# Identity products in TensorE's waits of the first slots, and a rounding that needs one PSUM bank

## The chip, the cores and the metric

The kernel runs on one core of a Trainium2 chip. The metric is device time in microseconds of one execution, as the median of several runs. The engines are TensorE (PE for its products, PEld for its weight loads), VectorE (DVE), ScalarE (ACT), GpSimd (POOL) and SyncE (SP), which here only issues DMAs. [...]

## The reference

Two layers in a row, in f32. The first is a recurrence of 768 steps on a 40 x 40 state for each of 4 x 8 heads; the second is a feed-forward network (FFN) with squared ReLU on the 3072 tokens that come out.

```python
for t in range(S):                                   # S = 768, B = 4, H = 8, D = 40
    y[:, :, t] = np.einsum('bhd,bhde->bhe', rt, state)
    Sa = np.einsum('bhde,bhe->bhd', state, at)
    state_decay = state * wt[:, :, None, :] - np.einsum('bhd,bhe->bhde', Sa, bt)
    state = state_decay + np.einsum('bhd,bhe->bhde', vt, kt)
...
x = np.ascontiguousarray(attn_out.transpose(0, 2, 1, 3)).reshape(B * S, H * D)   # 3072 x 320
h = np.maximum(x @ w_in, 0.0)                        # w_in 320 x 2048
return (h * h @ w_out).astype(np.float32)            # w_out 2048 x 320
```

The two weight matrices are made from random numbers times a factor, so they are f64: two 32-bit words for each element. The other inputs are f32.

## The kernel before

The recurrence is cut into chunks of 128 steps: 6 chunks for each of 4 batches, 24 in all, taken in the order of `order` (all batches of a chunk first). Within a chunk the steps are solved together, which needs the inverse of a triangular 128 x 128 matrix for each head.

For a chunk, `early` (or `prepare` around it) turns w, b and a on TensorE (`turn`, line 318), makes running products of w by scans and two reciprocals on VectorE (lines 354 to 360), multiplies (366, 367) and makes the matrices N with products of 40 rows (`products`, line 326). ScalarE copies them to SBUF (375 to 379), and they are stored in DRAM. GpSimd fetches them (`take`), inverts small triangles step by step (`solving`, lines 442 to 452), and stores the result as kept_t (455). `inverses` fetches that back as blocks (472), and joins it into T: a transpose on VectorE (484), two rounds of 32 x 32 products on TensorE, copies on ScalarE (486, 496, 503). `chain` is the recurrence proper: in_v,A products, then xr,T and minus_x,N products by turns with ScalarE's copies between, a transpose (635), the masked RX (645), and the products that make the tokens (661) and the new state. `turn_rv`, `make_rv`, `turn_k`, `turn_down` and `scale_kb` prepare r, v and k for it; `turn_down` transposes the decays, and VectorE multiplies k and b by them (552).

A slot is the work on one chunk woven with the preparation of others. Slots 0 to 3 are `opening_slot`, which has no FFN in it; from slot 4 on it is `sorted_slot`, with the FFN's steps between: `thirds` and `whole` (the first layer: w_third and w_in products into two ps_f banks), `square` (line 726) and `make_quarter` (the second layer). After slot 23 `rest` does what is left of the FFN. The order of all engines' work is the order in which these steps are called. `later`, `tick` and `flush` delay the issue of stores and fetches by a number of steps; nearly all of them go through SP's queue, and GpSimd issues its own.

The weights come as f64 and are rounded to f32 on the chip by `rounding`, in 26 pieces: 10 of 512 columns (w_in and w_third) and 16 of 320 (w_out). The raw words are fetched into lent space in SBUF (w_out's place, the hidden tiles). For each piece ScalarE turns the low words into a fraction (line 264); VectorE takes the exponent (277) and the mantissa (278) from the high words into two PSUM banks and adds the fraction (279); in the next step ScalarE makes a power of two of the exponent (260), and VectorE puts in the sign (268) and multiplies (269). Then a further fetch may use the raw space (`then`, line 239). `thirds` may start when the first 10 pieces are done, and `make_quarter` when all are. The pieces are dealt to the slots by `pieces_in` (line 867): 3, 6, 6 and 9 in slots 0 to 3, and 3 in slot 4, the last of which only ends the piece before.

[...]4 in the pool ps_w, 2 in ps_c, and 2 in ps_f, which the rounding uses until slot 4 and the FFN after it:

```python
bits, mant = (psum(ps_f)[:, :dst.shape[-1]] for _ in range(2))
```

Ahead of the loop, the first four chunks are prepared (`e0` to `e3`), the first chunk's own preparation is `r0`, and `solve` 0, 1 and 2 are GpSimd's first three units, of 1, 1 and 2 chunks.

## Time and profile before

| | us |
|---|---|
| median of 3 runs (lowest, highest) | 973.73 (973.63, 974.14) |
| the profiled execution | 973.32 |
| its span, first to last instruction | 971.5 |

| engine | busy, us | share of the span | instructions |
|---|---|---|---|
| PE | 874.8 | 90% | 9008 |
| PEld | 725.8 | 75% | 9008 |
| DVE | 477.4 | 49% | 872 |
| ACT | 284.7 | 29% | 735 |
| POOL | 512.4 | 53% | 993 |

| stretch, us | PE busy | DVE busy | granted PE clock |
|---|---|---|---|
| 50 to 100 | 34.19 | 27.36 | 0.57 |
| 100 to 150 | 32.82 | 38.21 | 0.60 |
| 150 to 200 | 39.63 | 39.04 | 0.59 |
| 200 to 250 | 29.69 | 31.35 | 0.69 |
| 250 to 300 | 47.40 | 28.81 | 0.97 |
| 300 to 350 | 48.83 | 29.16 | 1.00 |

Slot 0 begins with the join of T for chunk 0 at 58.7 us, slot 1 at about 91 us, slot 2 at 130, slot 3 at 170, and slot 4 at 214.5, as the transposes of in_r show; the first FFN product comes at 230.0. In the profile a group is named by its output and inputs, so "PE ps_w L318" is a transpose into a bank of the pool ps_w, and "ps_c<-xr,T" a product whose operands are xr and T. An f32 product is two PE instructions. The granted clock is the share of full speed at which TensorE's array was allowed to run.

### The profile page before, as it was taken

The numbers are of one execution on the slowest core, as the hardware profiler recorded it, in microseconds if no ns is written. First come the engines' busy times: TensorE is split into PE (matmuls) and PEld (weight loads), VectorE is DVE, ScalarE is ACT, GpSimd is POOL, SyncE is SP. The second block draws the span as 40 slices with busy tenths as digits, with TensorE's granted clock in tenths as the row PEclk, the third lists the DMA queues.
The fourth block names the chain that finished last, engine by engine and source line by source line (L and its number), as shares of the span: only waits on it lengthen the run. The fifth ranks groups of instructions, "written<-read, shape, count | busy, mean of one in ns | idle before, by whom it ended". The sixth has DMA issues, their size and how long they took to land.

```text
span 971.5 us, 22220 instructions
## 1 busy us (share of the span) xinstructions
PE 874.8 (90%) x9008; PEld 725.8 (75%) x9008; DVE 477.4 (49%) x872; ACT 284.7 (29%) x735; POOL 512.4 (53%) x993
## 2 busy tenths in 40 slices
PE   6457856755989999999999999999999999999998
PEld 4446745654868878788878888888888888887776
DVE  5527975876466556536644644644334323231111
ACT  3133432433332423323323422222222221222111
POOL 4788327064183846029999739999858860000000
PEclk9856565566999999999999999999999999999999
DMA  8989997874566897884772796525454353130000
GB/s 101 147 167 142 173 173 174 185 136 85 100 116 117 148 170 134 145 152 87 120 109 70 147 157 118 107 44 85 98 118 80 55 107 67 32 51 8 14 14 13
DMA packets 256313, 103.67 MB, mean 107 GB/s; under 512 B 237236, under 2 KB 243252, under 8 KB 255060
## 3 DMA queue, kind: packets, MB, share of 16 engines
q1 hardware_dynamic: 251892, 86.92, 51.4%
q0 software_dynamic: 3232, 15.21, 6.9%
q8 instruction: 71, 1.16, 0.5%
q10 hardware_dynamic: 1088, 0.13, 0.1%
q14 instruction: 30, 0.25, 0.1%
HBM read 69.33 MB, written 30.92 MB: 103 GB/s over the span
## 4 chain that ended last, share of the span: by engine, by line
PE 75%; DVE 8%; DMA 5%; issue 4%; SPq 3%; POOL 3%; ACT 2%; DVEq 0%; ACTq 0%; POOLq 0%
PE ps_f L87 40%; PE ps_w L87 15%; PE ps_c L87 12%; PE ps_w L318 5%; DMA blocks<-kept_t 2%; PE ps_c L635 1%; PE ps_c L562 1%; POOL half_t L452 1%; POOL half_p L450 1%; SPq L144 1%; PE ps_w L546 1%; DVE decay L359 1%; DMA kept_q<-N 1%; DMA kept_t<-half_t 1%; DMA w_out<-in_moe_w_in_dram 1%
## 5 line engine op out<-in xcount | busy, mean ns | idle before, releaser
L450 POOL TENSOR_TENSOR half_p<-half_n,half_t 128x126 f32<-128x126 f32 (+44 forms) x437 | 225.0, 515 | 95.2 <-DMA half_n<-kept_q 30.2
L452 POOL TENSOR_TENSOR half_t<-half_t,half_p 128x126 f32<-128x126 f32 (+44 forms) x437 | 241.9, 553 | 34.2
L87 PE MATMUL ps_f<-w_out,hid 128*128 128x320 f32 x768 | 222.5, 442 | 0.0
L87 PEld LDWEIGHTS ps_f<-w_out,hid 128*128 128x128 f32 x768 | 143.8, 193 | 54.8 <-issue 2.5
L87 PE MATMUL ps_f<-tokens,w_in 128*128 128x256 f32 x672 | 156.9, 387 | 0.0
L87 PEld LDWEIGHTS ps_f<-tokens,w_in 128*128 128x128 f32 x672 | 126.2, 193 | 17.8 <-issue 1.0
L726 DVE TENSOR_TENSOR hid<-hid 128x512 f32<-128x512 f32 x96 | 81.5, 886 | 50.2 <-ACT hid L719 49.7
L719 ACT ACTIVATE hid<-ps_f 128x512 f32<-128x512 f32 x84 | 50.2, 597 | 86.1 <-PE ps_f L87 86.1
L422 POOL DMA_DIRECT2D half_n<-kept_q x18 | 9.4, 528 | 102.6 <-DMA kept_m<-N 55.4
L661 DVE TENSOR_TENSOR tokens<-ps_c,dec 128x512 f32<-128x512 f32 x24 | 16.6, 691 | 90.2 <-PE ps_c L87 90.2
L354 DVE TENSOR_TENSOR_SCAN decay<-ps_w,ones 128x64 f32<-128x64 f32 x88 | 23.9, 272 | 72.8 <-PE ps_w L318 72.8
L87 PE MATMUL ps_w<-decay,bT 40*128 40x128 f32 x352 | 31.7, 314 | 26.4 <-DVE decay L367 26.1
L87 PE MATMUL ps_f<-tokens,w_third 64*128 64x256 f32 x336 | 46.6, 385 | 8.0 <-DVE w_out L268 8.0
L87 PEld LDWEIGHTS ps_w<-decay,bT 40*128 40x128 f32 x352 | 28.6, 219 | 30.4 <-DVE decay L367 21.7
L375 ACT COPY N<-ps_w 128x256 f32<-128x256 f32 x48 | 17.7, 369 | 112.4 <-PE ps_w L87 69.9
L512 DVE TENSOR_TENSOR kvT<-ps_w,dec 128x512 f32<-128x512 f32 x24 | 16.5, 687 | 68.8 <-ACT minus_x L622 34.4
L334 DVE TENSOR_TENSOR RV<-ps_w,upper 128x512 f32<-128x512 f32 x48 | 30.9, 686 | 38.8 <-PE ps_w L87 38.5
L334 DVE TENSOR_TENSOR RX<-ps_w,upper 128x512 f32<-128x512 f32 x48 | 30.8, 684 | 35.4 <-PE ps_w L87 35.2
L87 PEld LDWEIGHTS ps_c<-xr,T 64*64 64x64 f32 x768 | 29.9, 146 | 19.9 <-issue 15.3
L87 PE MATMUL ps_w<-spares 32*32 32x32 f32 x448 | 11.9, 208 | 32.9 <-DVE spares L484 17.5
L87 PEld LDWEIGHTS ps_f<-tokens,w_third 64*128 64x128 f32 x336 | 31.7, 190 | 10.3 <-DVE w_out L268 8.3
L87 PE MATMUL ps_c<-xr,T 64*64 64x40 f32 x768 | 35.9, 240 | 2.7 <-ACT xr L629 1.6
(130 smaller groups left out, 1422.9 us busy)
## 6 DMA issues: line engine op xcount, KB each, us to landing
kept_e<-decay SPq DMA_DIRECT2D x22, 633.8 KB
dec<-kept_e SPq DMA_DIRECT2D x22, 633.8 KB
hid<-in_moe_w_out_dram SPq DMA_DIRECT2D x16, 320.0 KB
in_w<-in_w_dram SPq DMA_DIRECT2D x24, 160.0 KB
in_ab<-in_b_dram SPq DMA_DIRECT2D x24, 160.0 KB
in_ab<-in_a_dram SPq DMA_DIRECT2D x24, 160.0 KB
in_k<-in_k_dram SPq DMA_DIRECT2D x24, 160.0 KB
in_r<-in_r_dram SPq DMA_DIRECT2D x24, 160.0 KB
```

Source lines behind the costliest of these rows:

```text
L87: nc.tensor.matmul(o, l_, r_, start=start, stop=True, skip_group_check=True)
L144: nc.sync.dma_start(out=t_[:, :, :D], in_=src[bb, :, c * C:(c + 1) * C, :].rearrange("h t d -> t h d"))
L318: nc.tensor.transpose(p_[:, q * 128:(q + 1) * 128], pair(x_, q), ident)
L334: nc.vector.tensor_tensor(t_, p_, over4(upper), Alu.mult)
L354: nc.vector.tensor_tensor_scan(up[:, q, MID + 1:C + 1], wT[:, q, MID:], ones, 1.0, Alu.mult, Alu.mult)
L375: nc.scalar.copy(plain, p_[:, ::2].rearrange("s h (f t) -> s f h t", f=2))
L450: nc.gpsimd.tensor_tensor(p_, part[:, at:at + m_].unsqueeze(1).to_broadcast([128, n, m_]), t3[:, :n, s:s + 1].to_broadcast([128, n, m_]), ...
L452: nc.gpsimd.tensor_tensor(t3[:, :n, s + 1:], t3[:, :n, s + 1:], p_, Alu.subtract)
L512: nc.vector.tensor_tensor(kT, kT_, down[:, :, 1:C + 1], Alu.mult)
L661: nc.vector.tensor_tensor(t_, y_, g["up"][:, :, :C], Alu.mult)
L719: nc.scalar.activation(h_, p_.rearrange("p f t -> p (f t)"), Act.Relu)
L726: nc.vector.tensor_tensor(h_, h_, h_, Alu.mult)
```

## The change

A new function, `fill_in(cols)`, issues products of the identity with itself, repeated along the columns, up to 4 x 128 columns in one product, into a PSUM bank that nobody reads. It is called 7 times ahead of the loop, 5 times in each opening slot, and twice in slot 4 (B is 4). Its bank, and one for the rounding, are taken once from the pool ps_f, so the rounding has one bank where it had two: the mantissa goes into the low words of the raw data in SBUF, the sum is made in place in the destination, and the sign is put into the bank instead of the destination.

```diff
+    bits_bank, fill_bank = psum(ps_f), psum(ps_f)
+
+    def fill_in(cols):
+
+        while cols:
+            n = min(4, cols)
+            nc.tensor.matmul(fill_bank[:, :n * 128], ident, ident.unsqueeze(1).to_broadcast([128, n, 128]),
+                             start=True, stop=True, skip_group_check=True)
+            cols -= n
+
     def rounding():
...
             if before:
-                d_, hi, mant, bits = before
-                nc.vector.scalar_tensor_tensor(d_.bitcast(I32), hi, -(1 << 31), bits, Alu.bitwise_and, Alu.bitwise_or)
-                nc.vector.scalar_tensor_tensor(d_, mant, 2.0 ** -20, d_, Alu.mult, Alu.mult)
+                d_, hi, bits = before
+                nc.vector.scalar_tensor_tensor(bits, hi, -(1 << 31), bits, Alu.bitwise_and, Alu.bitwise_or)
+                nc.vector.scalar_tensor_tensor(d_, d_, 2.0 ** -20, bits.bitcast(FP32), Alu.mult, Alu.mult)
...
                 hi = words[:, :, 1].bitcast(I32)
-                bits, mant = (psum(ps_f)[:, :dst.shape[-1]] for _ in range(2))
-                bits = bits.bitcast(I32)
+                low, bits = words[:, :, 0].bitcast(I32), bits_bank[:, :dst.shape[-1]].bitcast(I32)
                 nc.vector.tensor_scalar(bits, hi, 20, 0x7FF, Alu.logical_shift_right, Alu.bitwise_and)
-                nc.vector.tensor_scalar(mant.bitcast(I32), hi, 0xFFFFF, 0x100000, Alu.bitwise_and, Alu.bitwise_or)
-                nc.vector.tensor_tensor(mant, mant.bitcast(I32), dst, Alu.add)
-                now = dst, hi, mant, bits
+                nc.vector.tensor_scalar(low, hi, 0xFFFFF, 0x100000, Alu.bitwise_and, Alu.bitwise_or)
+                nc.vector.tensor_tensor(dst, low, dst, Alu.add)
+                now = dst, hi, bits
...
+    fill_in(4)
     go(e0, 3)
     go(e1)
+    fill_in(4)
     go(e0)
...
     go(e1)
+    fill_in(3)
     go(r0, 2)
...
     go(e3, 2)
+    fill_in(10)
     go(e2)
     go(e3, 2)
+    fill_in(14)
     flush()
     join = inverses(0, ready[0])
     go(join)
     go(e3)
+    fill_in(52)
     flush()
     solve(1, {8: lambda: weights_by(0, nc.gpsimd), 20: lambda: take(2, own)})
...
         fill("f")
+        fill_in(4)
         if j == 2:
             join()
         step(of(turn_k))
         step(on(ch))
+        fill_in(2)
         step(of(turn_down), of(scale_kb), pieces)
...
         step(lambda: begin_chain(j, n))
+        fill_in(12)
         fill("n")
+        fill_in(4)
         if late:
             join()
         step(pieces)
+        fill_in(3)
         if late:
             join()
...
         step(of(turn_rv), on(one), on(one))
+        if i == B:
+            fill_in(10)
         fetch_next(j + 1, "r")
         step(second.make_quarter, pieces)
         step(on(ch), of(decay_state))
+        if i == B:
+            fill_in(10)
         step(pieces, of(make_rv), second.thirds)
```

## The prediction

> **What bounds the kernel now.** I read the page first, then the chain of waits, then stretches of 10 us, then the timelines of TensorE, VectorE, ScalarE and the SP queue from 0 to 300 us.

> ```profile
> PE   6457856755989999999999999999999999999998
> DVE  5527975876466556536644644644334323231111
> POOL 4788327064183846029999739999858860000000
> PEclk9856565566999999999999999999999999999999
> ```

> Each digit is a slice of 24.3 us. From the tenth slice on (about 230 us) PE is full and its clock granted in full: the tail is TensorE's own work, which the change doesn't touch. Before that PE is half busy at half clock, and something else sets the pace. What, differs from place to place:

> ```profile
> 76.75 3.44 DMA kept_t<-half_t
> ...
> 106.04 0.69 DVE RV L334
> 106.78 1.11 PE ps_w L318 x4
> ...
> 132.13 7.36 SPq L144
> ...
> 229.49 0.50 DVE w_out L268
> 230.04 2.59 PE ps_f L87 x7
> ```

> That is the chain (start, us, what). Up to 91 us it is GpSimd's solves and their round trips through DRAM; in slot 1 (91 to 130) VectorE, busy 93% of the time from 100 to 130, much of it with the rounding; in slot 2 (130 to 153) the SP queue, which waits 7.36 us for TensorE's in_ab transposes; then TensorE and VectorE in turn; in slots 3 and 4 mostly VectorE's rounding, until the last w_out piece lets the FFN start at 230.

> The clock matters more finely than in slices:

> ```profile
> 74.88:78.30 3.42, 3.42 (x34) 3.20 (x32) 2.72 (x5) 0.00 (x0) 2.57 (x10) 0.50 1.15 148
> 78.30:81.70 3.40, 3.40 (x52) 3.40 (x48) 2.44 (x4) 1.24 (x2) 2.54 (x9) 0.50 0.33 60
> 81.70:81.80 0.10, 0.10 (x8) 0.10 (x6) 0.00 (x0) 0.00 (x0) 0.10 (x2) 0.88 0.49 83
> 88.50:88.60 0.10, 0.10 (x4) 0.06 (x1) 0.00 (x0) 0.00 (x0) 0.05 (x1) 0.76 1.72 182
> 119.20:119.30 0.10, 0.10 (x6) 0.10 (x4) 0.10 (x1) 0.10 (x1) 0.00 (x0) 0.65 1.42 277
> 122.70:126.10 3.40, 0.00 (x0) 0.00 (x0) 3.26 (x7) 0.72 (x2) 0.00 (x0) 1.00 0.95 194
> 126.00:126.10 0.10, 0.00 (x0) 0.00 (x0) 0.10 (x1) 0.10 (x1) 0.00 (x0) 0.99 0.07 26
> 238.70:238.80 0.10, 0.10 (x2) 0.06 (x2) 0.00 (x0) 0.00 (x0) 0.00 (x0) 0.81 0.00 0
> ```

> The columns are stretch, length, PE, PEld, DVE, ACT, POOL, clock, DMA share, GB/s. The last column but two of each short stretch dates a change within it: 81.72, 88.55, 119.27, 126.10 and 238.74. The gaps are 2, 9, 2 and 33 times 3.413 us. [...]78.3 to 81.7, filled with RX and in_v,in_k products, raised it; 74.9 to 78.3, PE also "busy", did not[...].[...] The first 30 us show 1.0 only for want of a record: the in_ab transposes take 421 ns at 5 us and 273 ns after 245, so TensorE is cold there too.

> [...]here windows full of transposes (214.8 to 218.2) do raise the clock, so I count them. [...]the trace shows the hid squares (L726, two SBUF inputs) at a median of 687 ns from 245 to 300 us but 1204 ns from 400 to 500, where GpSimd's operations are larger.

> **The fills, price.** A filling product is a full f32 product of 128 rows. The tokens,w_in products (8 of 256 columns, 3.46 us warm) give 1.69 ns a column: 0.216 us for each unit of 128 columns warm, 0.432 cold. There are 87 units ahead of the loop, 25 in each of slots 0 to 3, 20 in slot 4: 207, or 45 us warm and 89 cold. Nothing reads the bank, so each costs only what TensorE would have done sooner.

> **Ahead of the loop.** The first 4 (1.73 cold) fit between ident (2.55) and in_w (4.24); they overrun by 0.1 at most. [...]the next 4 lie in the idle 2.57 before 11.44. Then the first N products (2.13 us on the chain, cold) take about half: -1.0, and GpSimd's whole row of solves starts that much sooner. The 3 lie in an idle 1.33; 10 (2.2) in 3.0 at 32 us; 14 (3.0) in 3.7; 52 (11.2) in 15.4. Unknown: whether 4 units hold the clock to 11.4. Bounds -1.2 to +0.3; I take -1.0.

> **Slot 0.** The 4 and 2 in its middle are cold, 2.6 us, and together with three dense transposes raise the clock some 7 us sooner, but slot 1 waits for GpSimd's blocks at 91: 0. The 12+4+3 at the end lie in waits and leave TensorE warm at 92.

> **Slot 1.** The 4 hide in the 2.26 us for RV; the 2 sit before turn_down's transposes, whose products VectorE waits for (L552, 0.52 idle now): +0.3 at most. Warm products spare its waits of 0.65 (A) and some tenths: -0.7. VectorE has nothing else to gain. -0.4.

> **Slot 2.** The 19 units at the end of slot 1 run as one block (4.1 warm) from 122, then TensorE idles to 130 for blocks: [...]cold at 130 as now. The in_ab transposes that the SP queue waits for end at 139.7 unchanged; the queue then issues for 14 us whatever TensorE does. [...]154.5 to 167 stays cold. 0; bounds -4 (warm from 130: half of 9.2 busy) to +0.5.

> **Slot 3.** The 19 units before it move its in_r and in_v transposes from 170 to about 174.7. ScalarE takes them in order: its rT copy starts at 174.52 now behind the rounding's two steps, so it waits 0.1 to 0.3, and the minus_x copy and the rounding behind it likewise; VectorE hardly. In the middle, 4 and 2 cost up to 2.6 cold beside in_k, xnT and dec transposes, which are followed by VectorE's kvT and L552; the same dense stretch raises the clock at 184 to 187.5 in place of 197.8. VectorE's waits from 189 to 196 are 1.40 (RX), 1.04 (A) and 1.02 (scans), 3.5 in all, and nearly go. Bounds -3.5 to +2.2; I take -2.2, some of the cost being felt.

> **Slot 4.** The 12 at the end of slot 3 hide in 9.9 us of idle time, but are over seven us before the N products at 212.5, which stay cold. 7 units then stand before in_r and in_v (3.0 cold); ScalarE's rT copy starts at 219.65 now and they end at about 219. The two tens take 2.2 each, warm after 218; rT,kvT ends at about 225.7, and the FFN waits for the rounding until 230. [...]the FFN starts cold and rises at about 238, as now. 0; bounds -4.4 (warm at once: half of 8.7 busy us) to +2.6.

> **The rounding.** As many instructions as before, 5 on VectorE and 2 on ScalarE for each of 26 pieces. Line 278 into SBUF at a stride of two words: L268 wrote SBUF at 676 to 690 ns, L277 PSUM at 684: equal. It must now follow ScalarE's read of the low words (L264), which ends over a microsecond earlier. Line 279 with two SBUF inputs: between 0 and +0.2 (L726's 892 ns maximum from 300 to 400 us, against 687) for each, 5 at most; I take +0.3 in all. The first FFN bank now comes free with L269, not L268: +0.5 at 230.

> **Sum.** -1.0 -0.4 -2.2 +0.3 +0.5 = -2.8 on the profiled execution's 973.32 (span 971.5 and 1.8 around it): 970.5; the median of the runs lies 0.4 above: 970.9.

> **The rivals.**
> 1. The clock holds into the FFN, or slot 2 starts warm: another -4.4 or -4, about 966.5. For: the tens are just ahead of it. Against: the 4.3 us gap.
> 2. Absorbed: VectorE at 93%, GpSimd and the SP queue keep their times and the gains in slot 3 are eaten by the fills there: 973.5.
> 3. Slower: [...]the fills run cold on TensorE's path. Slot 1 pays 0.85, slot 3 2.2; in slot 4, from 212.5, 2.1 products, 3.0 and 8.6 of fills and 6.4 of slot work end at 232.6, past the 230 at which the FFN is free: 2.6. With 0.5 for the bank, +6.2: 979.9.[...]
> 4. That it doesn't do what it says: products of an identity might not count as activity. It gives rival 3's time.

> **How the numbers follow.** Mine 0.41, rival 1 0.17, rival 2 0.22, rivals 3 and 4 together 0.20. About 0.2% (2 us) is what a measurement can tell here. Faster: 0.32 of mine, 0.17, and 0.03 of rival 2: 0.52. Same: 0.08 and 0.16: 0.24. Slower: 0.01, 0.03 and 0.20: 0.24. My own range is 968 to 974; with the rivals, and the bounds of slots 2 to 4, 964 to 977.5.

> **What would show it.** Right: the clock at 1.0 from about 7 us and again from the middle of slots 0, 1 and 3; GpSimd's first half_p sooner than 24.84; VectorE's waits for RX, A and scans in slot 3 gone; first FFN product at about 227.5, still at 0.5. Wrong: RV products or turn_down late behind fills with VectorE idle; L279 well over 0.7; FFN start after 230; or the clock full there.

## The result, and the profile after

Twenty runs of the changed kernel took a median of 971.5 us (968.33 to 975.91). Twenty runs of the kernel before beside them took 973.08 us (968.24 to 976.97). The ratio is 0.9987, with a 95% interval of 0.9974 to 1.0. That is 0.13% faster, inside what I had called "no change", and the interval just reaches 1. The same kernel timed again later gave 971.43 us (14 runs) and a ratio of 0.9989 (0.9973 to 1.0005). Over all 34 runs of the changed kernel the median is 971.5; over 147 of the kernel before it is 972.7. (One further run of the kernel before fell into a slower state, 1452.05 us, and is left out.) So the change gains about 1.2 to 1.6 us, and single runs of it scatter over some 10.

The two profiled executions differ by more: 969.89 us after (span 968.2) against 973.32 (span 971.5), which is 3.4.

The slices of the changed kernel's page (tenths of busy time, 24.2 us each) show what it set out to do:

```profile
PE   6967975878989999999999999999999999999998
DVE  5527974876556556535655644643334323231111
POOL 4788518054182855039999749999768850000000
PEclk9869755978989999999999999999999999999999
```

TensorE is fuller in six of the first nine slices. The clock is up most in the fourth (0.6 to 0.9, slot 0), the eighth (0.5 to 0.9, slot 3) and the tenth (0.6 to 0.8, slot 4 and the FFN's start), and a little in the third, fifth and ninth. In the sixth and seventh, which are slot 2 for the most part, it stays at a half. The price stands in one group of the page (instructions, busy us and mean ns, then the idle time ahead of them):

```profile
L259 PE MATMUL ps_f<-ident 128*128 128x512 f32 (+2 forms) x114 | 56.9, 635 | 2.6 <-POOL ident masks.py:199 2.6
```

A product of f32 shows as two instructions, so these are 57 products (23 of them from six calls ahead of the loop, not seven as I wrote above), and 56.9 us of TensorE's time bought a gain of 1 to 2. The chain that ended last, in the changed kernel (start, us, what):

```profile
82.63 6.28 DMA blocks<-kept_t
...
133.12 4.58 SPq L144
137.75 4.47 SPq L144
...
228.79 2.07 PE ps_f L87 x6
231.87 5.02 PE ps_f L87 x16
```

It is the same chain in the same places: a round trip through DRAM ahead of slot 1, the SP queue in slot 2 (9.05 us in two DMAs where one took 7.36), and the FFN's first products at 228.79 instead of 230.04. The clock, in stretches (length, PE, PEld, DVE, ACT, POOL busy, clock, DMA share, GB/s), of the kernel before:

```profile
74.90:88.00 13.10, 9.72 (x132) 9.17 (x130) 10.27 (x17) 1.67 (x3) 10.68 (x33) 0.74 0.82 135
182.00:196.00 14.00, 13.27 (x128) 11.58 (x128) 10.32 (x24) 6.38 (x18) 0.00 (x0) 0.50 0.67 168
228.00:240.00 12.00, 9.96 (x48) 7.71 (x50) 7.03 (x10) 2.62 (x7) 2.06 (x7) 0.55 0.56 79
```

and of the changed one:

```profile
74.90:88.00 13.10, 12.05 (x168) 9.60 (x166) 10.43 (x19) 3.10 (x8) 10.83 (x31) 1.00 0.85 142
154.00:168.00 14.00, 11.48 (x133) 10.24 (x135) 10.55 (x24) 6.38 (x19) 11.67 (x30) 0.50 0.79 195
182.00:196.00 14.00, 12.51 (x154) 10.02 (x154) 12.09 (x31) 6.65 (x19) 0.28 (x1) 0.79 0.77 189
228.00:240.00 12.00, 11.21 (x68) 8.72 (x69) 5.47 (x7) 3.15 (x8) 3.32 (x12) 0.72 0.52 77
```

In slot 0 the clock is full earlier, with no gain; from 154 to 168 in slot 2 it stays at a half, as forecast; from 182 to 196, in the middle of slot 3, it is full for more than half of the time, and VectorE does 12.09 us of work there instead of 10.32. The waits of VectorE from 182 to 200 say the same. Of the kernel before (engine, what waits, for what: us, times, longest):

```profile
DVE RX L334 <- PE ps_w L87: 1.4, 1, 1.4
DVE A L334 <- PE ps_w L87: 1.0, 1, 1.0
DVE decay L354 <- PE ps_w L318: 1.0, 1, 1.0
```

of the changed one:

```profile
DVE A L343 <- PE ps_w L87: 1.2, 1, 1.2
DVE decay L363 <- PE ps_w L327: 0.4, 1, 0.4
DVE RX L343 <- PE ps_w L87: 0.2, 1, 0.2
```

3.4 us of waits have become 1.8 (1.9 in a second profile of the changed kernel). The waits for RX and for the scans shrank; the one for A did not. Where the profiled pair's 3.3 us of span went can be laid out by four landmarks that both timelines have. Three of them, of the kernel before:

```profile
154.50 1.42 PE L87 MATMUL ps_w<-spares 32*32 32x32 f32 x32 [7.47 <-DVE bT L366]
212.53 2.08 PE L87 MATMUL ps_w<-decay,bT 40*128 40x128 f32 x16 [9.93 <-DVE decay L367]
247.31 1.06 PE L87 MATMUL ps_c<-rT,sd 128*128 128x128 f32 x8
```

and of the changed one:

```profile
156.07 1.17 PE L87 MATMUL ps_w<-spares 32*32 32x32 f32 x32 [9.76 <-DMA spares<-kept_m]
211.01 2.08 PE L87 MATMUL ps_w<-decay,bT 40*128 40x128 f32 x16 [6.45 <-DVE decay L376]
244.37 1.06 PE L87 MATMUL ps_c<-rT,sd 128*128 128x128 f32 x8
```

The fourth is the FFN's first unbroken products (230.04 and 228.79). The columns give the length of each stretch:

| stretch | before | after | difference |
| --- | --- | --- | --- |
| start to the spares products that open slot 2's second half | 154.50 | 156.07 | +1.57 |
| from there to the N products at slot 3's end | 58.03 | 54.94 | -3.09 |
| from there to the FFN's first unbroken products | 17.51 | 17.78 | +0.27 |
| from there to the first rT,sd products | 17.27 | 15.58 | -1.69 |
| from there to the end | 724.19 | 723.83 | -0.36 |

This is one pair of executions. The second profile of the changed kernel, shown further on, has landmarks that lie over 2 us from those of the first.

### The profile page after: what moved, and what is told of

It is laid out like the page before. It is cut to its first block, busy times and chain, and to the rows that moved or that the text cites. A ratio compares the mean times of both kernels' runs of the same rounds, so it can differ in the third digit from the quotient of the medians.

```text
span 968.2 us, 22417 instructions
## 1 busy us (share of the span) xinstructions
PE 905.3 (94%) x9122; PEld 728.9 (75%) x9122; DVE 471.2 (49%) x872; ACT 285.4 (29%) x735; POOL 518.2 (54%) x993
## 4 chain that ended last, share of the span: by engine, by line
PE 79%; DVE 9%; DMA 3%; issue 3%; SPq 2%; ACT 2%; POOL 2%; ACTq 0%; DVEq 0%; POOLq 0%
PE ps_f L87 40%; PE ps_w L87 16%; PE ps_c L87 12%; PE ps_w L327 6%; PE ps_c L644 1%; PE ps_c L571 1%; DVE decay L368 1%; PE ps_w L555 1%; SPq L144 1%; PE ps_f L259 1%; DMA blocks<-kept_t 1%; DVE ps_f L286 1%; DVE decay L363 1%; DVE hid L735 1%; DVE ps_f L278 1%
## 5 line engine op out<-in xcount | busy, mean ns | idle before, releaser
L459 POOL TENSOR_TENSOR half_p<-half_n,half_t 128x126 f32<-128x126 f32 (+44 forms) x437 | 229.0, 524 | 96.6 <-DMA half_n<-kept_q 30.5
L87 PE MATMUL ps_f<-w_out,hid 128*128 128x320 f32 x768 | 221.3, 440 | 0.0
L87 PEld LDWEIGHTS ps_f<-w_out,hid 128*128 128x128 f32 x768 | 142.9, 191 | 54.3 <-issue 1.4
L87 PE MATMUL ps_f<-tokens,w_in 128*128 128x256 f32 x672 | 155.7, 385 | 0.0
L87 PEld LDWEIGHTS ps_f<-tokens,w_in 128*128 128x128 f32 x672 | 125.3, 191 | 17.5 <-issue 1.0
L735 DVE TENSOR_TENSOR hid<-hid 128x512 f32<-128x512 f32 x96 | 78.8, 857 | 50.2 <-ACT hid L728 49.8
L259 PE MATMUL ps_f<-ident 128*128 128x512 f32 (+2 forms) x114 | 56.9, 635 | 2.6 <-POOL ident masks.py:199 2.6
L87 PE MATMUL ps_f<-tokens,w_third 64*128 64x256 f32 x336 | 46.7, 383 | 3.9 <-DVE w_out L279 3.9
L87 PEld LDWEIGHTS ps_c<-xr,T 64*64 64x64 f32 x768 | 29.5, 144 | 19.4 <-issue 15.5
L87 PE MATMUL ps_w<-decay,bT 40*128 40x128 f32 x352 | 28.8, 295 | 14.1 <-DVE decay L376 13.5
L543 DVE TENSOR_TENSOR f<-end,dec 128x4 f32<-128x4 f32 x20 | 6.1, 307 | 71.3 <-DMA dec<-kept_e 71.3
L87 PEld LDWEIGHTS ps_w<-decay,bT 40*128 40x128 f32 x352 | 26.0, 201 | 19.4 <-DVE decay L376 17.1
L259 PEld LDWEIGHTS ps_f<-ident 128*128 128x128 f32 x114 | 22.3, 214 | 21.1 <-issue 17.8
```

The lines of the kernel that those rows point to most:

```text
L87: nc.tensor.matmul(o, l_, r_, start=start, stop=True, skip_group_check=True)
L259: nc.tensor.matmul(fill_bank[:, :n * 128], ident, ident.unsqueeze(1).to_broadcast([128, n, 128]), start=True, stop=True, skip_group_check= ...
L459: nc.gpsimd.tensor_tensor(p_, part[:, at:at + m_].unsqueeze(1).to_broadcast([128, n, m_]), t3[:, :n, s:s + 1].to_broadcast([128, n, m_]), ...
L735: nc.vector.tensor_tensor(h_, h_, h_, Alu.mult)
```

## The experiments

My theory: the gain comes from slot 3 alone, in which VectorE waited for cold products; everything ahead of it is taken back by DRAM round trips and a full DMA system (a DMA share of 0.96 from 128 to 140 in the kernel before) before slot 2's second half; and the gaps that no filling product covers (slot 2, the end of slot 3, just before the FFN) are what limits the change. The rivals: that the rounding gives the time (or costs more than it seems), that the solves ahead of the loop start sooner and carry the gain through, and that slot 2 waits for TensorE's cold transposes. Twelve kernels, one of them the change itself, were run in three groups, each with the kernel before beside it (medians 972.61, 972.9 and 972.6 us; a ratio is always to that). All edits are to the changed kernel.

**The rounding alone.** No filling product is issued.

```diff
-        while cols:
+        while cols and False:
```

> The rounding as changed, with no fills: VectorE and ScalarE do the same number of operations, and the FFN's second bank comes free half a microsecond later. Prediction's terms: +0.3 for line 288 and +0.5 for the bank, so 0.8 us slower than before, first FFN product near 230.8. Rival[...]: line 288 well over 0.7 us for 512 columns and 3 to 5 us slower. Rival (the rounding itself is what gained): faster by 1 us or more, FFN start before 229.

973.11 us, ratio 1.0009 (0.9996 to 1.0022): half a microsecond slower than before, within the interval of nothing. The new rounding gives nothing that the runs can tell, and costs little. Its profile has 18.07 us from slot 3's N products (211.91) to the FFN (229.98) where the kernel before has 17.51, +0.56: about the half microsecond that the bank was to cost. The next two kernels, which have no fills in slot 4 either, have 18.06 and 18.08 there. The composition of VectorE's part is another than I had thought. VectorE's groups up to 235 us (busy us and mean ns, then the idle time ahead), before:

```profile
L279 DVE TENSOR_TENSOR ps_f<-ps_f,w_out 128x320 f32<-128x320 int32 x16 | 8.0, 500 | 1.7
L278 DVE TENSOR_SCALAR ps_f<-hid 128x320 int32<-128x320 int32 x16 | 7.7, 484 | 0.0
L278 DVE TENSOR_SCALAR ps_f<-w_out 128x512 int32<-128x512 int32 x8 | 5.5, 684 | 0.0
```

and in the changed kernel, where they are lines 288 and 287:

```profile
L288 DVE TENSOR_TENSOR w_out<-hid,w_out 128x320 f32<-128x320 int32 x16 | 8.5, 531 | 0.5
L287 DVE TENSOR_SCALAR hid<-hid 128x320 int32<-128x320 int32 x16 | 5.2, 325 | 0.0
L287 DVE TENSOR_SCALAR w_out<-w_out 128x512 int32<-128x512 int32 x8 | 3.3, 418 | 0.0
```

The sum with two SBUF inputs takes 31 ns more; the step that now writes SBUF takes 159 and 266 ns less. VectorE's busy time falls from 477.4 to 474.1 us over the kernel with the rounding alone, and the kernel did not become faster by it.

**The fills ahead of the loop alone**, switched off at the loop's start:

```diff
+    filling = [True]
...
-        while cols:
+        while cols and filling[0]:
...
+    filling[0] = False
```

> Only the 87 units ahead of the loop, with the rounding as changed. The prediction's step: the first N products 1 us sooner, GpSimd's row of solves 1 us sooner, and so the whole 1 us faster than the rounding alone. Theory after the trace of the changed kernel: N is 0.7 us sooner, but two round trips through DRAM on a full DMA system take it back before the first half_p (24.8), and slots 0 to 2 are paced by the DMA queue, so the time equals that of the rounding alone within 0.5 us and the joins of slots 0, 1 and 2 are where they were.

972.93 us, 1.0004 (0.9994 to 1.0013). Against the rounding alone that is -0.2. The 87 units ahead of the loop do nothing that can be measured, though the two intervals are too wide to exclude a gain of 1 us.

**The fills of slot 3 alone**: from the 12 at the end of slot 2 to the last ones of slot 3.

```diff
+        filling[0] = i in (2, 3)
         fill_in(12)
...
+        filling[0] = i == 3
```

> Only the fills from the end of slot 2 to the end of slot 3 (12, 4, 3, then 4, 2, 12, 4, 3), with the rounding as changed. Theory: from the N products of slot 2 (154.5 before) to those at the end of slot 3 (212.5) the kernel is no longer paced by DMA, and this is where TensorE's clock is worth something: 58.0 us of it become 55, and the whole is 2 us faster than the rounding alone, as fast as the full change. Rival (the gain is spread over all fills, or lies in slot 4's): less than 1 us of the gain is here.

971.06 us, 0.9988 (0.9978 to 0.9998): the whole gain of the change, and 2.05 below the rounding alone. From 182 to 196 its clock is at 0.74, where the rounding alone has 0.50 throughout:

```profile
182.00:196.00 14.00, 12.50 (x149) 10.82 (x149) 10.45 (x26) 6.93 (x19) 1.32 (x3) 0.74 0.73 182
```

Its N products come at 210.09 (211.91 with the rounding alone) and its FFN at 228.17 (229.98), both 1.8 sooner. So 44 units of the 207 carry the change; the whole change, at 971.5, is no faster than this. Its own profiled span, 970.8, shows almost none of that (971.3 with the rounding alone): from its first rT,sd products at 243.81 it took 727.0 us to the end, where the rounding alone took 724.5 from 246.84. One span is not enough to tell two microseconds, and neither is one landmark or one stretch. The kernel with the fills ahead of the loop has none in slot 3, and yet its profile has

```profile
182.00:196.00 14.00, 11.77 (x146) 10.29 (x144) 10.63 (x26) 6.27 (x18) 0.00 (x0) 0.69 0.77 193
```

and took 55.77 us from slot 2's second half to the N products; this kernel took 55.98. What separates the two sorts is all profiles together. From slot 3's in_r transposes to its N products the mean granted clock is 0.63, 0.65 and 0.74 in the three kernels without fills in slot 3, and 0.80 to 0.90 in the eleven profiles with them. VectorE's waits for TensorE, from slot 2's second half to those N products, are 5.4 to 6.9 us in the three and 2.1 to 5.7 in the eleven. This kernel's own waits hardly fell (5.5 us; from 182 to 200 RX's went, while A took 1.6 and the scans 1.0). So the runs show that the gain comes with slot 3's fills; that it comes through VectorE's waits is what most profiles suggest, and this one doesn't.

**Bridge from slot 1 to slot 2.** 24 more units behind the block at the end of slot 1, so that slot 2 starts warm.

```diff
-        fill_in(3)
+        fill_in(3 + (24 if i == 1 else 0))
```

> The full change with 24 more units (5.2 us at full clock) ahead of the join of slot 2, so that TensorE enters slot 2 at full clock and does 130 to 140 in about half the time. The prediction took the SP queue's long issue there (7.36 us) for a wait for TensorE's in_ab transposes: then this gives 3 to 4 us. Theory now: the queue is held by a full DMA system, not by TensorE; the second half of slot 2 (spares products at 156 in the changed kernel) starts where it did, and the time is the changed kernel's within 1 us, though the in_ab transposes of slot 2 come 4 us sooner.

970.65 us, 0.9985 (0.9972 to 0.9998): the change's own time within the intervals. The clock stood at 1.00 from 128 to 140 (in the changed kernel it fell at 125.38), as a stretch of this kernel shows:

```profile
128.00:140.00 12.00, 8.10 (x147) 6.12 (x146) 8.65 (x16) 8.36 (x20) 1.81 (x5) 1.00 0.90 210
```

The in_ab transposes came 6.06 us after the spares products that open slot 2 (7.8 in the changed kernel). The SP queue was no sooner for it (start, us, line, operation):

```profile
135.83 6.55 SPq L144 DMA_DIRECT2D in_w<-in_w_dram  x1
...
143.85 6.33 SPq L110 DMA_DIRECT2D tokens<-tokens  x8
...
153.70 1.27 SPq L488 DMA_DIRECT2D spares<-kept_m  x2
```

The second half's first products then stood as late as ever:

```profile
156.51 1.14 PE L87 MATMUL ps_w<-spares 32*32 32x32 f32 x32 [9.34 <-DMA spares<-kept_m]
```

That speaks against the reading that TensorE holds up the SP queue in slot 2. The queue spends 6.55 us on one DMA whose issue began after the in_ab transposes were done (at 135.56). The kernel before says the same: its 7.36 us (DMA share 1.03) belong to the fetch of in_w, whose last readers on TensorE had ended 11 us earlier:

```profile
120.38 0.66 PE L318 MATMUL ps_w<-ident,in_w 128*128 128x128 f32 x4
132.13 7.36 SPq L144 DMA_DIRECT2D in_w<-in_w_dram  x1
```

In the fourteen profiles, slot 2's second half starts at 154.1 to 157.5 us, whether slot 2 opened at 126 or at 130. What holds the queue was not shown; I ran no kernel with fewer transfers.

**Bridge within slot 2**, after its transposes, over the stretch that stayed at half clock:

```diff
         step(of(turn_down), of(scale_kb), pieces)
+        fill_in(36 if i == 2 else 0)
```

> The full change with 36 more units (7.8 us at full clock) in the middle of slot 2, where TensorE idles from 146 to 156 for spares, so that the work from 156 to 168 runs at full clock. Theory: this stretch waits for TensorE (RX 1.5 us, A 1.0 us and more on VectorE), no longer for DMA, so 2 to 3 us less than the changed kernel. Rival (slot 3's first half is paced by VectorE's rounding and by DMA, such as in_k, anyway): TensorE is done sooner but the N products of slot 3's end stay where they were, within 1 us.

969.44 us, 0.9955 (0.9939 to 0.997). The clock from 154 to 168 rose from 0.50 to 0.77, and the stretch from the second half to slot 3's N products fell from 54.94 to 52.65 us (156.44 to 209.09). VectorE's waits for TensorE in that stretch are 2.1 us, the least of all profiles. The interval lies just under the change's (0.9974 to 1.0).

**Bridge from slot 3 to slot 4**, over the idle 6 to 10 us ahead of the N products:

```diff
-        fill_in(12)
+        fill_in(12 + (24 if i == 3 else 0))
```

> The full change with 24 more units (5.2 us) at the end of slot 3, so that the N products there run at full clock. ScalarE's N copies and the rounding queue behind these products. Theory: products 1.16 us in place of 2.08, so the rounding of slot 4 and the FFN come 0.9 us sooner. Rival: a filling that ends late delays the N products, 0 or slower.

969.53 us, 0.9959 (0.9946 to 0.9973). The N products and the transposes behind them now run warm, the clock from 205 to 215 being 1.00 (0.61 in the changed kernel), and the scatter of the runs is small (967.85 to 971.99). The profiled FFN start, 229.06 and cold, isn't sooner, so where on the path the gain arises isn't shown.

**The clock held to the FFN.** Twenty units between the last rT,kvT products of slot 4 and the FFN's first ones:

```diff
-        step(pieces, of(make_rv), second.thirds)
+        step(pieces, of(make_rv), lambda: fill_in(20 if i == B else 0), second.thirds)
```

> The full change with 20 more units (4.3 us at full clock) right ahead of the FFN's first products in slot 4, where TensorE idled 3.9 us and lost its clock. Theory: the FFN then starts at full clock; from its first product to the rT,sd products it takes 13 us in place of 15.6, and the time is 2 to 3 us less than the changed kernel's, about 4 us less than before. Rival (the FFN's start is paced by something else, such as its weights or ScalarE): the stretch stays above 15 us and the time stays within 1 us of the changed kernel's.

967.31 us, 0.993 (0.9905 to 0.9955), about 4 us under the change. The timeline of TensorE in the changed kernel (start, us, instructions, and the idle time ahead with what ended it):

```profile
224.33 0.59 PE L87 MATMUL ps_f<-tokens,w_third 64*128 64x256 f32 x2
228.79 2.07 PE L87 MATMUL ps_f<-tokens,w_third 64*128 64x256 f32 x6 [3.86 <-DVE w_out L279]
...
231.80 5.09 PE L87 MATMUL ps_f<-tokens,w_in 128*128 128x256 f32 x16
```

and in this one:

```profile
223.42 4.56 PE L259 MATMUL ps_f<-ident 128*128 128x512 f32 x10
228.29 1.13 PE L87 MATMUL ps_f<-tokens,w_third 64*128 64x256 f32 x8 [0.31 <-DVE w_out L279]
...
229.95 3.72 PE L87 MATMUL ps_f<-tokens,w_in 128*128 128x256 f32 x16
```

The fill lies wholly in the wait for the rounding (VectorE's L279 ends it), and the same 16 products take 3.72 us warm where they took 5.09 partly cold. From the FFN's first products to rT,sd it is 12.86 us (15.58 in the changed kernel, 17.27 before). The runs scatter widely, though (961.95 to 970.56).

**The three bridges together** (slot 2, slot 3 to 4, FFN):

> All three additions together (20 ahead of the FFN, 36 in slot 2, 24 at the end of slot 3). Theory: their gains add, 4 to 6 us less than the changed kernel, 966 us. Rival (each only moves the wait to DMA or to VectorE's rounding): the sum is no more than the best of them alone.

965.55 us, 0.9919 (0.9896 to 0.9942). The clock of this kernel:

```profile
205.00:215.00 10.00, 8.69 (x44) 5.00 (x43) 5.79 (x14) 4.23 (x13) 8.35 (x22) 1.00 0.75 122
228.00:240.00 12.00, 12.00 (x96) 10.42 (x95) 4.53 (x5) 4.93 (x11) 3.12 (x11) 1.00 0.31 44
```

It is full in both stretches, and the FFN starts at 226.77:

```profile
219.76 4.56 PE L259 MATMUL ps_f<-ident 128*128 128x512 f32 x10
226.77 1.14 PE L87 MATMUL ps_f<-tokens,w_third 64*128 64x256 f32 x8 [2.45 <-DVE w_out L279]
```

The 36 units in slot 2 didn't hold it in this profile (0.52 from 154 to 168).

**The same without the 36 units of slot 2:**

> The change with the fills ahead of the FFN (20) and at the end of slot 3 (24), without the 36 in slot 2. Theory: in the three bridges TensorE's clock was 0.52 from 154 to 168, so the 36 units were of little use there, since DMA's lateness varies and the clock is lost before the work comes: within 1 us of the three bridges. Rival: slot 2's fill was worth the 2 us that it showed by itself: 2 us slower than the three bridges.

967.39 us, 0.994 (0.9923 to 0.9956). That is 1.8 above the three, but the intervals meet, so what slot 2's bridge adds to the others stays open. Its profile shows how narrow the thing is:

```profile
223.19 4.56 PE L259 MATMUL ps_f<-ident 128*128 128x512 f32 x10
229.80 1.92 PE L87 MATMUL ps_f<-tokens,w_third 64*128 64x256 f32 x8 [2.05 <-DVE w_out L279]
...
232.66 5.76 PE L87 MATMUL ps_f<-tokens,w_in 128*128 128x256 f32 x16
```

The fill ended 2.05 us before the FFN could start; the clock fell at 230.0, and all but the first 0.2 us of the FFN's first 7 ran at half clock (0.72 from 228 to 240). (The profiled run took 971.5, the most of the six; the least is 964.35.) The kernel with three bridges stood idle 2.45 us in the same place and kept its clock (1.00 from 228 to 240).

**The three bridges without the fills ahead of the loop and in slots 0 and 1:**

> The three bridges without any fill ahead of the loop or in slots 0 and 1. Theory: up to the middle of slot 2 the DMA queue sets the pace, so those 137 units are worth nothing and the time equals that of the three bridges within 1 us. Rival: the sooner N products and the warm slot 1 are worth the 1.4 us that the prediction gave them, and this is slower by it.

967.49 us, 0.995 (0.9935 to 0.9966), 1.9 above the three bridges with them. Its profile, again of the run that took most (971.7), lost the clock at the FFN after an idle 2.09 us (0.76 from 228 to 240). That those early fills are worth nothing is therefore not confirmed: alone they gave nothing, and here the intervals meet. It isn't settled whether they help or whether this is the FFN's lot drawn differently.

**The change again**, in the same group as the last kernels, to see how far a second timing agrees:

> The changed kernel itself, unaltered, beside the others on one chip. From the parts (rounding alone +0.5, ahead of the loop -0.2, slot 3 -1.9 against the rounding): 1.5 us less than before, ratio 0.9985, and the same landmarks as in its first profile within 2 us. If its first timing was a poor draw and the added terms of the prediction hold, 2.8 us less.

971.43 us, 0.9989 (0.9973 to 1.0005): it agrees. Its profile has slot 2's second half at 154.14, N at 208.55, the FFN at 226.38 and a span of 967.2; the first one had 156.07, 211.01, 228.79 and 968.2. So one kernel's landmarks move by over 2 us from one execution to another.

**Further fills in slots 4 to 7**, added to the three bridges, where the FFN's products run out for a moment. The FFN holds both banks of ps_f by then, so `fill_in` takes a bank of ps_w as a second argument here:

```diff
-        step(second.make_quarter, on(two))
+        step(second.make_quarter, lambda: fill_in(8 if i < 2 * B else 0, psum(ps_w) if i < 2 * B else None), on(two))
```

> The three bridges, and 8 units (1.7 us at full clock, into a bank of the pool that the products use next) in each of the waits of 2.5 us for the decays in slots 4 to 7, after which some profiles show 3.4 us of half clock (276 to 280 before). Theory: such a half-clock stretch costs up to 1.7 us where the grid falls badly, so 0.5 to 3 us less than the three bridges and a smaller spread. Rival: these waits are mostly survived as it is, and a fill that overruns delays the N products: no change or 1 us slower.

963.63 us, 0.9907 (0.9891 to 0.9923). With the three bridges there was still a stretch at half clock in the tail:

```profile
262.00:292.00 30.00, 27.49 (x283) 22.16 (x284) 16.87 (x31) 9.36 (x26) 21.20 (x56) 0.89 0.62 118
```

Here it is gone:

```profile
262.00:292.00 30.00, 29.06 (x307) 23.66 (x306) 17.96 (x31) 12.39 (x36) 19.84 (x52) 1.00 0.60 114
```

All five of its runs (961.87 to 964.68) lie under all fourteen of the change in that group (967.25 to 977.28). It is the fastest version of this study and beats both kernels; its step over the three bridges (-1.9) is within their intervals.

## Why the prediction came out as it did

The direction held, and so did the place of the gain, slot 3. The size came out at about half: -2.8 us was forecast, -1.2 to -1.6 measured. That 971.5 lies so near to 970.9 says little, as rival 2's 973.5, with the gains eaten up, is only 2.6 us from my forecast. By steps:

- **Ahead of the loop, -1.0: not borne out.** The first N copy did come 0.71 us sooner (12.84 against 13.55), behind warm products (the clock was 1.00 from 5.91 to 12.74). GpSimd's first half_p, which I had put "that much sooner", came at 24.77 against 24.84. Between the two lie two trips through DRAM: the kept_q issue was 0.71 sooner (14.60), the half_n load 0.32 (18.86), the solve 0.07. That is the first profile; in seven others with the N copy that early the solve starts at 23.99 to 24.44, so some half a microsecond often gets that far and is lost later. In the runs these fills alone gave -0.2, and the whole change is no faster than slot 3's fills alone.
- **Slot 0, 0: right.** The clock was full from 74.2 instead of 81.72, and slot 1's blocks came no sooner (92.26 against 91.74).
- **Slot 1, -0.4: not shown.** Slot 2 opened sooner (128.55 against 129.99) and its second half began later (156.07 against 154.50). But with the rounding alone, without any fill, slot 2 opened at 127.04, so the profiles do not tell slot 1's fills from chance.
- **Slot 2, 0: right in size, wrong in reason.** I wrote that the queue's 7.36 us "waits for TensorE's in_ab transposes". It is the issue of in_w's fetch, and the bridged slot 2 shows that it doesn't wait for them. The bound of -4 for a warm start, and with it half of rival 1, fell with that reading.
- **Slot 3, -2.2: right in size.** -2.05 in the runs against the rounding alone. Of the 3.5 us of waits that were to "nearly go", 1.6 went in the changed kernel's profile: RX's and the scans', and not A's.
- **Slot 4, 0: right.** The FFN started cold after 3.86 idle us. The bound of -4.4 for a warm start was also of the right size: about -4 between the medians, once a fill held the clock (in the profiles 12.86 us from the FFN's start to rT,sd instead of 17.27 before). That is the other half of rival 1, which needed 20 units more than the change has.
- **The rounding, +0.8: +0.5 in the runs**, with an interval from -0.4 to +2.1; its terms were off. I put line 278 into SBUF at "equal"; it saved 5.2 us of VectorE (16 times 159 ns, 8 times 266, 2 times 261), none of it seen in the time. Line 279 cost some 0.6 of VectorE rather than 0.3, which the runs can't resolve. The bank's +0.5 shows as +0.55 to +0.57 in three profiles against the one of the kernel before.

So the true sum is nearer to -2.05 + 0.5 = -1.5 than to -2.8, and the medians give -1.2 to -1.6. What is missing from the forecast is the two terms ahead of slot 2 (-1.4), which the runs don't show. The profiled pair came closer to -2.8 than the reasons deserve: -1.69 of its -3.3 lie behind the FFN's start, where its clock rose at 234.6, 5.8 us in, and in the kernel before at 238.74, 8.7 us in. Each of the two times lies a whole multiple of 3.413 us from every other change of the clock in its profile; where the FFN's start fell between such times is no step of mine.

Rival 2, absorbed, was half right: slots 0 to 2 did absorb their fills. It was wrong in slot 3. The median lies between its 973.5 and my 970.9, nearer to mine, but as the interval reaches 1 the whole change's ratio alone doesn't exclude it; the slot 3 run, with an interval under 1 throughout, speaks against it. Rival 3, cold fills on the path, did not decide; behind the mid-slot blocks of all four slots the clock rose to 1.00 (at 74.18, 108.31, 145.86 and 186.82), though in slot 2 it fell again at 149.27, in the idle time up to 156. With that, rival 4 fell too. The bridged slot 2 shows it best: TensorE ran 9.50 us of nothing but products of the identity, from 118.75, and the granted clock from 128 to 140 was 1.00.

## What to carry to other kernels

Work that only keeps a clock up paid here in two places: where TensorE's cold products stood between another engine and its data, and up to the very start of TensorE's own dense work. Look for those first. Gains ahead of a stage paced by transfers did not show in this kernel's time, so ask of each step what the next fixed point is. When an effect is a fifth of a per cent and runs scatter over one, read landmarks in several profiles and the medians of many runs; a single pair of spans or landmarks says little.
